# The last chunk's heads in other tiles, the rest behind the loop, paired convolution streams and another stage table, in a fused S4 convolution and multi-query attention kernel

## The chip, the cores and the metric

The kernel runs on one core of a Trainium2 chip. A core has a matmul engine (PE, with weight loads shown apart as PEld), a vector engine (DVE), an activation engine (ACT), a general engine (POOL) and a queue engine that mostly issues DMAs (SP). Each engine works through its own queue in program order; semaphores join them. Matmuls write to PSUM banks, everything else lies in SBUF or in DRAM. The metric is the device time of one execution in microseconds, the median of several runs.

## The reference

Two independent parts whose outputs are set side by side. Part A is a state-space (S4) convolution over 2048 positions and 576 channels; part B is attention with 32 heads of 18 columns that share one key and one value head.

```python
def _A_ref(u, A_re, A_im, B_re, B_im, C_re, C_im, log_dt, Dskip):
    ...
    P = jnp.exp(logdA[:, :, None] * l[None, None, :])
    K = jnp.einsum("dn,dnl,dn->dl", Cc, P, dB).real
    ...            # y: causal convolution of u with K, by FFT of length 2L
    return y + u * Dskip[None, None, :]

def _B_ref(x, wq, wk, wv, wo):
    ...            # q: 32 heads of 18; k, v: one head of 18
    scores = jnp.einsum("bhqd,bkd->bhqk", q, k) * (Dh ** -0.5)
    p = _softmax(scores, axis=-1)
    o = jnp.einsum("bhqk,bkd->bhqd", p, v)
    return o.transpose(0, 2, 1, 3).reshape(B, S, H * Dh) @ wo

return jnp.concatenate([a, b], axis=-1)
```

## The kernel before

**Attention** runs over 4 chunks (c) of 512 queries, in each over 8 groups (g) of 4 heads, in each over 16 key blocks (kb) of 128 keys: 512 steps. A step takes two pairs of heads: for each pair a score tile (`s`, two matmuls, L551) and one exponential on ACT (`P`, 128x1024, L562); then one *product* of four matmuls with the values (`ops`, L865), which also sums the softmax's denominators. Three score tiles (NS) and ten tiles of exponentials (NP) are in turn. After key block 15, `gather` copies the four heads to SBUF and stores them to `od` in DRAM (L571).

`normalize` turns a chunk's heads into normalised ones. For some of five column groups m (126 columns each, the last 72) it loads the denominators (`dn`, L584), takes reciprocals on DVE, stores them to `rden` (L588), loads the heads into tile `oT` (L591), loads the reciprocals broadcast over each head's 18 rows (`db`, L598) and multiplies (DVE). `outproj` then multiplies by `wo`: 8 sums (4 blocks of 128 queries by 2 column halves) over the five m. For the last chunk the projection is cut by m (`outproj_part`, after groups 1, 3, 5 and 6 by LATE): a sum over one m is taken in PSUM and collected by DVE in `part`. What is still in `self.rest` when the loop ends, and the last m by another route (`w4`, `b4`), is done by `finish`.

**The convolution** works through 12 blocks of 48 channels. `front(k)` builds tables of powers on DVE (`tab`) and from them the kernel on PE (`kg`, L1300), sent through DRAM (`kd`, `kt`). `back(k)` transforms input and kernel (`hu`, `lu`, `hk`, `lk`), multiplies on DVE (`acc`, `pt`), and transforms back (`iy`), after which block k is stored.

**What sets the order.** PE, ACT and DVE run in the order in which the program is written; DMAs on SP are placed by their dependences. `main` writes three scores, the exponentials, then products and *filler*: steps of four generators (`prep` for normalize, `tail`, `side` for query projections and outproj, and the convolution's streams). A clock inside the program (`K.t` for PE, `K.v` for DVE, `K.a` for ACT) estimates when each step could begin; `fill` takes those that fit before the next scores are due. The table `PLAN` gives the constants of this choice for each stage of 32 steps (RATE and PACE for the convolution's speed, TOTAL and LAST for how filler is spread over the steps, C1 to C12, and so on). A generator's `yield "v", t, ...` waits for that clock to reach t, `"p"` asks for PE, `"w"` waits for another generator. All filler sums go through one PSUM bank (`bank`), which DVE must empty before the next.

The places that the change touches: tile `oT` has one buffer, used by all chunks, so the last chunk waits in `prepare` until chunk 2's projection is done:

```python
            while ms[0] == 0 and (self.outs or c == NCH - 1 and self.due < 1 << 30):
                yield "w", 0.0, False
```

and the two convolution streams, `fronts` and `backs`, go on independently, where a stream that did vector work last goes first again:

```python
        for st in sorted(self.streams, key=lambda st: (not st.holds, st.kind == "v" and st is not self.on, st.work)):
```

Of the kernel before, what the change touches and what calls it, by code (L numbers as in the profile page):

```python
# [50 lines left out]
LAST = 405.243  # L51
# [3 lines left out]
    0: dict(RATE=1.916, PACE=1.819, AHEAD=0.674, TOTAL=358.207, GAP=0.333, DEFER=0.474, SLACK=3.538, HEAD=11.297, LEFT=1.367, C1=0.645, C2=0.912, C3=0.747, C4=1.053, C5=0.661, C6=1.093, C7=0.426, C8=0.221, C9=0.253, C10=0.689, C11=16.545, C12=15.321),  # L55
    1: dict(DEFER=0.444, SLACK=4.537, C10=0.575),
    2: dict(TOTAL=449.207, SLACK=4.082, HEAD=8.942),
    3: dict(RATE=1.877, TOTAL=358.207, SLACK=3.538, HEAD=11.297),
    5: dict(C11=19.186, C12=19.023),
    6: dict(RATE=1.952, C3=0.59, C4=1.266, C11=21.544),  # L60
    7: dict(RATE=1.916, C3=0.747, C4=1.053, C11=19.186),
    8: dict(LEFT=1.309, C5=0.644, C8=0.226, C9=0.311, C10=0.623),
    9: dict(RATE=1.906, DEFER=0.45, C3=0.831),
    10: dict(GAP=0.42, HEAD=12.368, C4=1.259, C8=0.182, C10=0.683),
    11: dict(RATE=1.916, GAP=0.291, DEFER=0.444, HEAD=13.273, C2=0.697, C3=0.747, C4=1.053, C8=0.208, C9=0.388, C10=0.557),
    12: dict(AHEAD=0.91, LEFT=1.367, C3=0.588, C5=0.661, C8=0.192, C9=0.316, C10=0.461),
    13: dict(AHEAD=0.701, GAP=0.333, C8=0.205, C9=0.332, C10=0.469),
    14: dict(PACE=1.844, AHEAD=0.86, C6=0.87),
    15: dict(RATE=1.869, PACE=1.922, AHEAD=0.657, GAP=0.384, DEFER=0.409, LEFT=1.696, C7=0.331, C8=0.169, C9=0.316, C10=0.408),
# [145 lines left out]
class Attention:  # L215
# [357 lines left out]
    def normalize(self, c, ms):  # L573
# [11 lines left out]
        yield "v", K.t + 8.0, False  # L585
# [3 lines left out]
        for m in ms:  # L589
            m0, mn = MT[m]  # L590
            nc.sync.dma_start(o[:mn, m, :], od[m0 // DH:(m0 + mn) // DH, 0:DH, :])  # L591
        yield "v", max(K.v, K.t) + 5.0, False
        tiles = {}

        def fetch(m):
            m0, mn = MT[m]
            tiles[m] = self.p1.tile([P, CT], F32, tag="db", name=f"db{c}_{m}", bufs=2)
            nc.sync.dma_start(tiles[m][:mn, :], rd[m0 // DH:(m0 + mn) // DH, :].unsqueeze(1).broadcast_to([mn // DH, DH, CT]))  # L598
        for m in ms[:2]:
            fetch(m)  # L600
        for m in ms:
            mn = MT[m][1]
            yield "v", K.t + 7.0, False
            V.tensor_tensor(o[:mn, m, :], o[:mn, m, :], tiles[m][:mn, :], op=ALU.mult)
# [4 lines left out]
    def outproj(self, c):  # L609
# [4 lines left out]
        for t in range(4):  # L614
# [17 lines left out]
            if t < 3:  # L632
                yield "p", K.fill, False

    def outproj_part(self, c, ms, part):

        nc, V, K = self.nc, self.V, self.k
        o = self.oT
        self.o_left += 8 * len(ms)
        for t in range(4):  # L640
            for n in range(2):
# [3 lines left out]
                for m in ms:  # L645
                    matmul4(nc, ps, o[:126, m, t * P:(t + 1) * P], self.wo[:126, m, cs], start=(m == ms[0]), stop=(m == ms[-1]))
# [13 lines left out]
    def finish(self, c, part, o_ps, w4, b4):  # L660


        nc, V, o = self.nc, self.nc.vector, self.oT
# [7 lines left out]
        def begin(t, nh, tile):  # L671

            ps[t, nh] = tile[:, :288]
            for m in range(4):
                if (t, nh, m) in self.rest:
                    matmul4(nc, ps[t, nh], o[:126, m, t * P:(t + 1) * P], self.wo[:126, m, cols[nh]], start=(m == min(x[2] for x in self.rest if x[:2] == (t, nh))), stop=False)
# [72 lines left out]
    def prepare(self):  # L749

        nc = self.nc
        while True:
# [5 lines left out]
            while ms[0] == 0 and (self.outs or c == NCH - 1 and self.due < 1 << 30):  # L758
# [3 lines left out]
            if c == NCH - 1 and ms[0] == 0:  # L762
                self.part = self.xp.tile([P, 4, D], F32, tag="x", name="part")
                self.rest = {(t, n, m) for t in range(4) for n in range(2) for m in range(4)}
            if ms[0] == 3:
                self.w4 = self.p1.tile([P, D], F32, tag="ob", name="w4")
# [857 lines left out]
```

## Time and profile before

| | |
|---|---|
| median of 3 runs | 1147.22 us (1146.74 to 1147.87) |
| the profiled execution, its own time | 1146.74 us |
| its span, first to last instruction | 1145.0 us |
| mean granted PE clock | 0.993 |
| first exponential begins / last ends | 25.9 us / 1109.0 us |
| exponentials | 1024, of 1036 ns (1121 ns for the first 32) |

The page has the busy share of each engine, the span in 40 slices, the chain of work that ended last, and the costliest groups of instructions; the trace behind it answers for any stretch. In a group's row stand line, engine, operation, `out<-in` by the program's names, count, then busy time and mean length of one, then the engine's idle time before it and what ended that. In a row of stretches stand the busy times of PE, PEld, DVE, ACT and POOL with their counts of instructions, the granted PE clock, the DMA share and GB/s. A matmul in 32-bit floats stands twice in the records. Idle time of an engine costs only where another waits for it.

```profile
PE   6989999999999999899999999999999999999986
DVE  3878998899999998999899999996998999994823
ACT  3889988988898999999899989999899999999970
```

### The profile page before, as it was taken

What the parts mean: (1) busy time and instruction counts of PE and PEld (TensorE: products, weight loads), DVE (VectorE), ACT (ScalarE), POOL (GpSimd) and SP (SyncE); (2) the same over time, 40 slices, a digit from 0 to 9 for tenths busy, and PEclk for the clock granted to TensorE, in tenths of its full rate; (3) what the DMA queues carried; (4) which work ended last, traced back from release to release, by engine and by line L of the source; (5) the groups of instructions that cost most, each with busy time, mean ns of one, the idle gap of its engine ahead of it and who ended that gap; (6) DMA issues with size and microseconds to landing.
All of it is one profiled execution on the core that took longest, in us unless ns stands there. A gap on an engine that the chain in (4) does not pass through costs nothing.

```text
span 1145.0 us, 33016 instructions
## 1 busy us (share of the span) xinstructions
PE 1082.4 (95%) x13886; PEld 395.8 (35%) x13886; DVE 991.3 (87%) x1676; ACT 997.1 (87%) x1052; POOL 139.5 (12%) x257
## 2 busy tenths in 40 slices
PE   6989999999999999899999999999999999999986
PEld 2333333334334333333333233333333233333323
DVE  3878998899999998999899999996998999994823
ACT  3889988988898999999899989999899999999970
POOL 5333212412122100000102010000020000000000
PEclk9999999999999999999999999999999999999997
DMA  7424142312214103031303112012132102011201
GB/s 225 142 58 125 40 146 62 113 42 82 62 58 158 43 22 103 20 111 37 108 29 124 46 34 87 29 38 71 40 128 72 59 23 95 29 43 43 79 34 53
DMA packets 59279, 83.37 MB, mean 73 GB/s; under 512 B 14867, under 2 KB 35335, under 8 KB 58613
## 3 DMA queue, kind: packets, MB, share of 16 engines
q1 hardware_dynamic: 47557, 73.24, 19.6%
q0 software_dynamic: 10848, 7.37, 2.6%
q8 instruction: 111, 1.82, 0.7%
q10 hardware_dynamic: 720, 0.58, 0.2%
q14 instruction: 43, 0.35, 0.1%
HBM read 46.59 MB, written 33.85 MB: 70 GB/s over the span
## 4 chain that ended last, share of the span: by engine, by line
PE 64%; ACT 14%; DVE 13%; issue 5%; DMA 2%; POOL 0%; SPq 0%; DVEq 0%; ACTq 0%
PE ops L865 26%; PE s L551 18%; ACT P L562 13%; PE op L212 5%; PE iy L212 3%; PE q L428 3%; PE kg L1300 2%; DVE tab L138 2%; DVE acc L138 1%; PE hk L212 1%; PE lu L212 1%; DVE ks L138 1%; PE fin L212 1%; PE hu L212 1%; DVE t L138 1%
## 5 line engine op out<-in xcount | busy, mean ns | idle before, releaser
L562 ACT ACTIVATE P<-s 128x1024 f32<-128x1024 f32 x992 | 933.1, 1036 | 88.1 <-PE s L551 86.0
L865 PE MATMUL ops<-P,v_sb 128*32 128x512 f32 x4096 | 504.1, 595 | 4.4 <-DVE o L142 4.0
L551 PE MATMUL s<-aug,kaug 55*128 55x512 f16 x2048 | 309.9, 380 | 25.6 <-ACT P L562 19.0
L551 PEld LDWEIGHTS <-kaug 55*128 55x128 f16 x2048 | 93.2, 94 | 352.8 <-issue 304.6
L865 PEld LDWEIGHTS ops<-P,v_sb 128*32 128x32 f32 x4096 | 117.0, 110 | 165.6 <-issue 136.4
L479 POOL DMA_DIRECT2D qd<-qh x116 | 66.1, 576 | 321.6 <-DVE qh L146 319.0
L428 PE MATMUL q<-x,wq_sb 128*32 128x256 f32 x1360 | 83.7, 383 | 1.2 <-issue 1.2
L212 PE MATMUL op<-wo_sb,oT 126*32 126x288 f32 (+1 forms) x1024 | 74.7, 418 | 2.8 <-DVE ob L142 1.6
L1211 POOL MEMSET fr<- 128x192 f32 x24 | 9.9, 494 | 442.5 <-DVE stage L138 237.8
L138 DVE TENSOR_TENSOR tab<-tab,tt 128x576 f32<-128x576 f32 (+1 forms) x72 | 59.2, 822 | 2.0
L138 DVE TENSOR_TENSOR tab<-fr,dif 128x576 f32<-128x576 f32 (+1 forms) x72 | 58.8, 817 | 0.0
L138 DVE TENSOR_TENSOR tab<-sum,fr 128x576 f32<-128x576 f32 (+1 forms) x72 | 58.7, 816 | 0.0
L138 DVE TENSOR_TENSOR tt<-fr,sum 128x576 f32<-128x576 f32 (+1 forms) x72 | 58.7, 816 | 0.0
L138 DVE TENSOR_TENSOR tab<-tab 128x576 f32<-128x576 f32 (+1 forms) x72 | 58.7, 815 | 0.0
L428 PEld LDWEIGHTS q<-x,wq_sb 128*32 128x32 f32 x1360 | 39.7, 109 | 37.2 <-issue 15.5
L138 DVE TENSOR_TENSOR acc<-acc,pt 128x1728 f32<-128x1728 f32 (+2 forms) x36 | 48.6, 1350 | 0.6
L138 DVE TENSOR_TENSOR pt<-us,ks 128x1728 f32<-128x1728 f32 (+2 forms) x36 | 47.8, 1350 | 0.2
L560 ACT ACTIVATE P<-s,bias 128x1024 f32<-128x1024 f32 x32 | 32.9, 1121 | 13.4 <-PE s L551 13.4
L1300 PEld LDWEIGHTS kg<-tab 128*32 128x32 f32 x2304 | 36.1, 110 | 21.1 <-issue 9.8
L1300 PE MATMUL kg<-tab 128*32 128x64 f32 x2304 | 41.8, 220 | 0.2
L138 DVE TENSOR_TENSOR ks<-ks 128x576 f32<-128x576 f32 (+1 forms) x48 | 41.0, 855 | 1.0
L212 PEld LDWEIGHTS op<-wo_sb,oT 126*32 126x32 f32 (+1 forms) x1024 | 29.1, 111 | 36.2 <-issue 13.4
(159 smaller groups left out, 995.0 us busy)
## 6 DMA issues: line engine op xcount, KB each, us to landing
od<-o SPq DMA_DIRECT2D x31, 256.0 KB
aug<-qd SPq DMA_DIRECT2D x124, 55.0 KB
u<-u SPq DMA_DIRECT2D x12, 384.0 KB
kd<-ksb SPq DMA_DIRECT2D x12, 384.0 KB
kt<-kd SPq DMA_DIRECT2D x48, 96.0 KB
outa<-u SPq DMA_DIRECT2D x12, 384.0 KB
pw<-pw SPq DMA_DIRECT2D x8, 528.0 KB
oT<-od SPq DMA_DIRECT2D x16, 252.0 KB
```

The source lines that it names most:

```text
L138: return self.v.tensor_tensor(out, *a, **k)
L212: nc.tensor.matmul(ps[j:e], w[:, j:e], x, start=start, stop=stop, tile_position=(0, j))
L428: nc.tensor.matmul(ps[o, 256 * f:256 * f + 256], w[:, k, i], xt[:, k, x], start=(k == 0), stop=(k == 4), tile_position=(0, 32 * j))
L479: q.dma_start(qd[h:h + n, row + d:row + d + nd, cs], src[i1:i1 + n * nd, :cs.stop - cs.start])
L551: nc.tensor.matmul(ps[:, j, :], self.kaug[r, kb * P:(kb + 1) * P], t[r, :], start=True, stop=True)
L560: nc.scalar.activation(pt, ps, AF.Exp, bias=self.bias, scale=SCALE / QQ)
L562: nc.scalar.activation(pt, ps, AF.Exp, scale=SCALE / QQ)
L865: nc.tensor.matmul(o_ps[32 * j:32 * j + 32, :], self.v[:, kb, :], pts[2 * n + j // 2][:, j % 2, :], start=(kb == 0), stop=(kb == 15), tile ...
L1211: nc.gpsimd.memset(t[:, :, 0:NF:8], one)
L1300: nc.tensor.matmul(ps[32 * g:32 * g + 32, d, :], t[:, :32], t[:, 32:], start=(j == 0), stop=(j == 1), tile_position=(0, 32 * g))
```

## The change

Four edits.

1. **Heads.** The last chunk's heads are no longer kept in `oT` but in the first four tiles of the query weights (`self.heads`, 512 columns of `wq[0]` to `wq[3]`), which are free once the last query projection is done. So the last chunk's normalisation waits for the queries alone, not for chunk 2's projection. `w4` is loaded when chunk 2's projection has been written. The waits in `normalize` are other ones: they reckon from the gather and from the time of the fetch.
2. **Behind the loop.** What is left after the last product is written in the order in which its inputs come by the program's clock.
3. **Streams in pairs.** Back of block k and front of block k + 1 make a pair of streams; the next pair begins when both are done. No stream keeps its turn.
4. **Stage table.** PLAN and LAST have other numbers.

```diff
-LAST = 405.243
+LAST = 576.841
...
-    0: dict(RATE=1.916, PACE=1.819, AHEAD=0.674, TOTAL=358.207, GAP=0.333, DEFER=0.474, SLACK=3.538, HEAD=11.297, ...
+    0: dict(RATE=1.86, PACE=1.856, AHEAD=0.729, TOTAL=340.0, GAP=0.359, DEFER=0.395, SLACK=3.285, HEAD=17.08, ...
...
-LAG = (0, -1)
...
@@ normalize
-        if ms[0] == 0:
-            self.oT = self.cp.tile([P, 5, CT], F32, tag="oT", name=f"oT{c}")
-        o = self.oT
+        if c < NCH - 1:
+            oT = self.oT = self.cp.tile([P, 5, CT], F32, tag="oT", name=f"oT{c}")
+            o = [oT[:, m, :] for m in range(5)]
+        else:
+            o = self.heads
...
-        yield "v", K.t + 8.0, False
+        yield "v", max(K.t + 1.0, self.o_free + 4.5) + 4.0, False
...
-        yield "v", max(K.v, K.t) + 5.0, False
-        tiles = {}
+        yield "v", max(K.v, K.t) + 1.6, False
+        tiles, fetched = {}, {}
...
-            yield "v", K.t + 7.0, False
+            yield "v", max(K.t, fetched[m] + 4.6), False
...
@@ outproj, at its end
+        if c == NCH - 2:
+            self.w4 = self.p1.tile([P, D], F32, tag="ob", name="w4")
+            nc.sync.dma_start(self.w4, self.a["wo4"])
...
@@ prepare
-            while ms[0] == 0 and (self.outs or c == NCH - 1 and self.due < 1 << 30):
+            while ms[0] == 0 and (self.outs if c < NCH - 1 else self.due < 1 << 30):
...
+                self.heads = [w.rearrange("p k n -> p (k n)")[:, :CT] for w in self.wq[:4]]
...
@@ main, behind the last product
-        while self.todo or self.busy or holder() or any(m == 0 for _, _, m in self.rest):
+        while True:
+            conv.turn()
+            h, live = holder(), [st for st in conv.streams if st.live]
             if self.todo or self.busy:
-                prep.advance()
-            elif holder() or self.outs:
-                (holder() or side).advance()
-        conv.drain()
+                live.append(prep)
+            if side.holds or self.outs and any(m == 0 for _, _, m in self.rest):
+                live.append(side)
+            if not live:
+                break
+            able = [st for st in live if st.kind == "v" or st.kind == "p" and h in (None, st)]
+            for st in [min(able, key=lambda st: st.event())] if able else live:
+                if st.live:
+                    K.t = max(K.t, st.event())
+                    st.advance()
...
@@ Conv
+    def turn(self):
+
+        if self.n < NCK and not any(st.live for st in self.streams):
+            self.n += 1
+            k = self.n
+            self.streams = [Stream(self.back(k, self.kt), self.k)] if k < NCK else []
+            if k + 1 < NCK:
+                self.streams.append(Stream(self.front(k + 1), self.k))
...
-        for st in sorted(self.streams, key=lambda st: (not st.holds, st.kind == "v" and st is not self.on, st.work)):
+        for st in sorted(self.streams, key=lambda st: (not st.holds, st.work)):
```

How the order of instructions moves, at three places.

On PE, from the last two products to the sums behind them. `fin` are the sums of `finish`, `bc` the broadcast of the last group's reciprocals; x24 are the 24 matmuls of six sums. Before:

```order
L865 MATMUL ops3_7_13947<-P3_14_15_14199,v_sb_115 32x512 x2
L865 MATMUL ops3_7_13947<-P3_15_15_14220,v_sb_115 32x512 x2
L212 MATMUL fin0_14263<-wo_sb_107,oT3_13810 32x288 x24
L704 MATMUL bc_14262<-rc_last_14261,b4_14246 128x256
L212 MATMUL fin1_14264<-wo_sb_107,oT3_13810 32x288 x24
L212 MATMUL fin2_14265<-wo_sb_107,oT3_13810 32x288 x24
L212 MATMUL fin0_14263<-w4_14245,o_last_14260 32x288 x8
L212 MATMUL fin3_0_14353<-wo_sb_107,oT3_13810 32x288 x12
```

Of the change:

```order
L869 MATMUL ops3_7_14039<-P3_14_15_14306,v_sb_115 32x512 x2
L869 MATMUL ops3_7_14039<-P3_15_15_14334,v_sb_115 32x512 x2
L211 MATMUL fin0_14358<-wo_sb_107,wq3_sb_105 32x288 x8
L211 MATMUL fin1_14359<-wo_sb_107,wq3_sb_105 32x288 x8
L211 MATMUL fin2_14360<-wo_sb_107,wq3_sb_105 32x288 x4
L709 MATMUL bc_14357<-rc_last_14356,b4_14032 128x256
L211 MATMUL fin2_14360<-wo_sb_107,wq3_sb_105 32x288 x4
L211 MATMUL fin0_14358<-w4_13157,o_last_14355 32x288 x8
L211 MATMUL fin3_0_14400<-wo_sb_107,wq3_sb_105 32x288 x4
```

Sums over m = 1 and m = 2 (16 of them) are gone from here; they stand as `op3_..._1` and `op3_..._2` in the last 23 groups of three scores.

On DVE, the last rows before the last group's reciprocal (`rc_last`). Before, with `db3_1` to `db3_3` the broadcast reciprocals of m = 1 to 3:

```order
L138 TENSOR_TENSOR oT3_13810<-oT3_13810,db3_1_14201 126x512
L146 TENSOR_SCALAR dn3_14_14235<-dn3_14_14235 28x128
L158 RECIPROCAL dn3_14_14235<-dn3_14_14235 28x128
L138 TENSOR_TENSOR oT3_13810<-oT3_13810,db3_2_14242 126x512
L146 TENSOR_SCALAR dn3_21_14249<-dn3_21_14249 28x128
L158 RECIPROCAL dn3_21_14249<-dn3_21_14249 28x128
L138 TENSOR_TENSOR oT3_13810<-oT3_13810,db3_3_14256 126x512
L938 TENSOR_SCALAR flag_58<-u2_3_4_11177 1x1
L693 TENSOR_SCALAR rc_last_14261<-ops3_7_13947 128x256
```

Of the change:

```order
L137 TENSOR_TENSOR wq3_sb_105<-wq3_sb_105,db3_3_14150 126x512
L137 TENSOR_TENSOR part_11912<-part_11912,op3_2_1_2_14216 128x288
L137 TENSOR_TENSOR w11_14185<-sv11_14184 128x2x192 x4
L137 TENSOR_TENSOR part_11912<-part_11912,op3_3_0_2_14245 128x288
L137 TENSOR_TENSOR u11_12556<-u11_12556,dsk11_12557 128x768
L137 TENSOR_TENSOR u11_12556<-u11_12556,iy110_14271 128x384
L137 TENSOR_TENSOR u11_12556<-u11_12556,iy111_14308 128x384
L137 TENSOR_TENSOR part_11912<-part_11912,op3_3_1_2_14340 128x288
L952 TENSOR_SCALAR flag_58<-u2_3_4_8890 1x1
L698 TENSOR_SCALAR rc_last_14356<-ops3_7_14039 128x256
```

The last head multiply moves ahead of the end of convolution block 11, and block 11's inverse transform (`iy11`), which stood ahead of the last fifteen products, now ends ahead of the last four.

On DVE, where block 10's products and block 11's tables meet. Before:

```order
L138 TENSOR_TENSOR pt10_2_13070<-us10_12300,ks10_12550 128x576
L138 TENSOR_TENSOR acc10_13004<-acc10_13004,pt10_2_13070 128x96x12
L138 TENSOR_TENSOR acc10_13004<-acc10_13004,pt10_2_13070 128x96x6
L138 TENSOR_TENSOR acc10_13004<-acc10_13004 128x768 x2
L138 TENSOR_TENSOR sv10_13128<-acc10_13004 128x384
L138 TENSOR_TENSOR sv10_13128<-acc10_13004 128x2x192
```

Of the change:

```order
L137 TENSOR_TENSOR acc10_13126<-acc10_13126,pt10_2_13305 128x96x6
L137 TENSOR_TENSOR tab11_1_13340<-sum11_12848,fr11_12677 128x24x24
L137 TENSOR_TENSOR acc10_13126<-acc10_13126 128x768
L141 COPY part_11912<-op3_2_0_0_13392 128x288
L137 TENSOR_TENSOR tt11_1_0_0_13343<-fr11_12677,sum11_12848 128x576
L137 TENSOR_TENSOR acc10_13126<-acc10_13126 128x768
L137 TENSOR_TENSOR tab11_1_13340<-tab11_1_13340 128x24x24
```

Rows of block 10 (`acc10`) and block 11 (`tab11`, `tt11`) now alternate, and a sum of the last chunk's projection (`part`) already stands among them.

More of the change, by code (lines that the diff above doesn't have):

```diff
@@ L1470, in early @@
         self.load(0)
[L1471 to L1482 removed]
+        self.n, self.burst = -1, False
+        self.streams = [Stream(self.front(0), self.k)]
     def begin(self, n):
@@ L1520, in drain @@
     def drain(self):
-        while any(st.live for st in self.streams):
-            for st in sorted(self.streams, key=lambda st: (not st.holds, st.kind == "w", st.work)):
+        while self.streams:
+            for st in sorted(self.streams, key=lambda st: (not st.holds, st.work)):
                 if st.live:
@@ L1525, in drain @@
                     break
+            self.turn()
 def build(tc, **aps):
```

72 lines of the change are left out of this document (29 added, 43 removed).

## The prediction

> **What bounds the kernel now.** First the page's head and its busy shares.
>
> ```profile
> span 1145.0 us, 33016 instructions
> PE 1082.4 (95%) x13886; PEld 395.8 (35%) x13886; DVE 991.3 (87%) x1676; ACT 997.1 (87%) x1052; POOL 139.5 (12%) x257
> ```
>
> No engine is the bound alone, and PE's 95% is not 5% of slack, because matmul ends are modelled. An average over the span hides where each is short, so I went to stretches: I cut the span at the first exponential of each 32 steps (64 exponentials a stage) and asked for each engine's busy time. Columns are start and end, length, then PE, PEld, DVE, ACT and POOL busy with their counts, granted clock, DMA share, GB/s. Four of the sixteen stages, and the sum of all:
>
> ```profile
> 242.40:314.20 71.80, 68.76 (x986) 27.02 (x987) 67.76 (x121) 60.46 (x66) 16.12 (x29) 1.00 0.24 69
> 381.80:445.20 63.40, 61.22 (x763) 21.21 (x752) 59.97 (x91) 59.98 (x66) 2.26 (x4) 1.00 0.15 45
> 853.60:914.30 60.70, 56.19 (x678) 18.08 (x678) 55.35 (x97) 59.55 (x65) 7.01 (x13) 1.00 0.21 67
> 1044.90:1109.00 64.10, 61.62 (x634) 19.89 (x635) 36.72 (x55) 60.16 (x64) 0.00 (x0) 1.00 0.15 50
> sum 1083.00, PE 1043.41 PEld 381.20 DVE 971.69 ACT 989.65 POOL 127.22; mean PE 65.21 PEld 23.83 DVE 60.73 ACT 61.85 POOL 7.95
> ```
>
> ACT needs about 60 us for any stage, and the lightest stage (853.6) takes hardly more. What a stage takes beyond that is ACT waiting for scores, because PE was busy with, or held up in, the other matmuls ("filler"). Over the loop this is 1083.0 - 989.65 = **93 us**. DVE is short in the early stages (67.76 of 71.80) and idles 27 us in the last (36.72 of 64.10).
>
> The loop's last exponential ends at 1109.0; the other 36 us lie behind it. Pieces of the chain in order of time (start, us, what) from there:
>
> ```profile
> 1108.08 1.35 DMA rden<-dn
> 1109.45 4.10 DMA db<-rden
> ...
> 1116.73 4.05 DMA db<-rden
> ...
> 1121.62 3.49 PE fin L212 x32
> 1125.12 0.63 PE bc L704 x2
> 1125.74 8.39 PE fin L212 x136
> ```
>
> The last chunk's heads of column groups m = 2 and m = 3 are normalised one after the other, each by a reciprocal, a store to DRAM and a broadcast load, while PE has nothing: `fin` cannot begin in earnest before 1121.62. Then 32 partial sums of the output projection, 24 of them over m = 1 to 3, run in the open.
>
> **The change part by part.** Times are against the profiled execution: span 1145.0, and 1.7 us around it (its own time is 1146.74; the median of the three runs, 1147.22, is 0.5 above). The rows of the end, from the timeline (start, us, engine, line):
>
> ```profile
> 1107.80 2.78 PE L865 MATMUL ops<-P,v_sb 128*32 128x512 f32 x24
> 1121.54 0.40 DVE L693 TENSOR_SCALAR rc_last<-ops 128x256 f32<-128x256 f32 x1
> 1121.98 1.75 DVE L696 RECIPROCAL rc_last<-rc_last 128x256 f32<-128x256 f32 x1
> 1125.78 0.42 DVE L690 TENSOR_TENSOR o_last<-o_last,bc 128x256 f32<-128x256 f32 x1 [1.77 <-PE bc L704]
> 1134.69 1.18 PE L212 MATMUL fin<-w,o_last 128*32 128x288 f32 x16
> 1138.49 1.55 DVE L682 TENSOR_TENSOR part<-part,fin 128x288 f32<-128x288 f32 x4 [1.74 <-PE fin L212]
> ```
>
> *1. Heads in their own tiles.* The last product ends at 1107.80 + 2.78 = 1110.6, so the tail is 1145.0 - 1110.6 = 34.4 us. In the change each m of the last chunk is normalised when its columns' groups are gathered, since it no longer waits for chunk 2's projection to leave oT; the multiply for m = 3 stands on DVE ahead of conv block 11's last transform, and `fin` holds 8 sums instead of 24. So the two round trips leave the tail, and 16 sums move into the loop. The new tail, from the end of the last product: DVE clamp 0.40 and reciprocal 1.75 (2.2; PE runs 5 sums of 0.49 beside it, 8.39 us for 136 records being 17 sums), bc 0.63, scale 0.42, the second reciprocal 1.75, bc 0.63, with some 0.4 of hand-over: 6.0. From there the rows of before run 1134.69 to 1140.04 = 5.35 with three sums in `begin(3,1)` where one is left (less 1.1): 10.25. From the last addition to the span's end before: 1145.0 - 1140.04 = 4.96. New tail **15.2, saved 19.2**. What is late next is DVE's pair of reciprocals, not PE.
>
> The saving includes a slow stretch of PE. By stretches:
>
> ```profile
> 1114.20:1124.40 10.20, 3.97 (x32) 1.39 (x36) 4.23 (x8) 0.74 (x2) 0.00 (x0) 0.50 0.08 27
> ```
>
> The granted clock was 0.50 there, behind the idle of 1111 to 1114, and 4 sums took 3.49 where four at 0.49 take 2.0. Without the idle I expect none of it.
>
> *2. The 16 sums in the loop.* Prices by the groups of the trace (busy over count, doubled, because a matmul stands twice in the records):
>
> ```profile
> L428 PE MATMUL q<-x,wq_sb 128*32 128x256 f32 x1360 | 83.7, 383 | 1.2 <-issue 1.2
> L212 PE MATMUL op<-wo_sb,oT 126*32 126x288 f32 (+1 forms) x1024 | 74.7, 418 | 2.8 <-DVE ob L142 1.6 <-DVE sck L138 1.2
> L1300 PE MATMUL kg<-tab 128*32 128x64 f32 x2304 | 41.8, 220 | 0.2
> L212 PE MATMUL iy<-w,dft_sb 128*32 128x192 f32 x768 | 37.3, 329 | 0.6 <-DVE ql L150 0.6
> L212 PE MATMUL hk<-kt,dft_sb 128*32 128x192 f32 x384 | 21.1, 331 | 1.6 <-DVE ql L150 0.8 <-DVE sck L138 0.5 <-PE s L551 0.3
> ```
>
> A sum of four is 8 records of op: 74.7 / 1024 x 8 = 0.58, so 16 are 9.3 us more filler in the loop. Bounds: nothing, if they fall where ACT is not kept waiting, and 9.3. The stages give the slope. Counted in the order and priced so, the filler of stage 242.4 was 25.4 us and ACT idled 71.80 - 60.46 = 11.3; stage 853.6 had 9.3 and idled 60.70 - 59.55 = 1.2; stage 381.8 had 14.8 and idled 3.4. From the first to the second that is 0.63 per us, thus +5.9; bent at the third it is 0.40 below 14.8 us and 0.75 above. **3. The stage table** shifts filler along that bend: by the same count stage 242.4 falls from 25.4 to 18.5 and stage 776.8 from 26.9 to 17.7, while stage 853.6 rises from 9.3 to 14.8 and the last from 14.8 to 23.2. Of the 9.3 us more, then, 5.5 lie below the bend (x 0.40) and 3.8 above it (x 0.75), together **+5**, which I take; 0 to 9.3 are the bounds.
>
> *4. Streams in pairs.* Back of block k runs beside front of k + 1 and neither keeps its turn, so DVE alternates between the two. From the DVE timeline:
>
> ```profile
> 1022.07 0.95 DVE L138 TENSOR_TENSOR tab<-fr,dif 128x768 f32<-128x768 f32 x1
> 1022.93 0.95 DVE L138 TENSOR_TENSOR tab<-sum,fr 128x768 f32<-128x768 f32 x1
> ...
> 1025.14 0.95 DVE L138 TENSOR_TENSOR tab<-tab 128x768 f32<-128x768 f32 x1
> 1026.12 0.96 DVE L138 TENSOR_TENSOR tab<-tab,tt 128x768 f32<-128x768 f32 x1
> ```
>
> Start to start is 0.86 where the next reads another tile and 0.98 where it reads the tile just written: 0.12 for the dependence. The order has 494 such neighbours before and 448 now: 46 x 0.12 = 5.5 us off DVE. Against it stand 16 additions into `part` at 1.55 / 4 = 0.39: 6.2. DVE's sum stays (+0.7); I count 0, bounds -2 to +3. [...]
>
> *5. Block 11 at the end.* Its transform back (iy11) now ends four products before the end instead of fifteen. Its chain before, from the DVE timeline:
>
> ```profile
> 1049.16 0.56 DVE L142 COPY sck<-hk 128x384 f32<-128x384 f32 x1 [2.80 <-PE hk L212]
> ...
> 1053.44 0.56 DVE L142 COPY sck<-hk 128x384 f32<-128x384 f32 x1 [1.72 <-PE hk L212]
> 1056.70 1.02 DVE L138 TENSOR_TENSOR sck<-lk,sck 128x384 f32<-128x384 f32 x2 [2.70 <-PE lk L212]
> ...
> 1080.51 1.00 DVE L138 TENSOR_TENSOR w<-sv 128x384 f32<-128x384 f32 x2
> ...
> 1113.57 0.69 DVE L138 TENSOR_TENSOR oT<-oT,db 126x512 f32<-126x512 f32 x1 [5.51 <-DMA db<-rden]
> ```
>
> From 1049.16 (its first kernel transform's copy) to 1081.5 (its last w) took 32.3 us with 4.4 us of waiting in it; that leaves 28 of work, to which the change adds ten additions (1.55 / 4 each: 3.9) and two head multiplies (0.69 each): 33.2. Between the same two places the new order has 36 exponentials, at 60.16 / 64 = 0.94 each 33.8 us. It fits with nothing to spare; PE waits in order at iy11. I add **+1**, bounds 0 to 8.
>
> *6. At no cost.* The dn, rden and db transfers of m = 0 to 2 lie under the loop; the new waits of the planner (8.5 us from gather to dn, 6.2 from reciprocal to multiply) cover the 5.45 us of the chain's first round (1.35 + 4.10). Without cover DVE waits for them, rival D. The new loop behind the last product finds no matmul left to place. w4 goes out earlier on SP. Sum: 1145.0 - 19.2 + 5 + 0 + 1 = 1131.8 span, **1133.5** with the 1.7.
>
> **The rivals.** *A, the forecast:* 1133.5, 1127 to 1141 by the bounds of parts 2 and 4. *B, DVE is relieved early:* block 11 ends 11 of 512 products later, so 2% of the 971.69 us of DVE work, some 20 us, leaves the first fourteen stages. If ACT's idle there falls by 0.4 of it, the loop is 8 us shorter: 1125.5. For it speaks that stages with DVE near its length idle most; against it that filler alone explains those stages. *C, DVE late at the end:* each addition frees the one filler bank, and the conv's long multiplies stand in front of some. If part 5 takes its 8 instead of 1: 1140.5. [...] *D, slower:* DVE, in order, stands at head multiplies whose broadcast has not landed, as it did 5.51 us ahead of the one at 1113.57. The place is the 19 multiplies in four chunks, where x of chunk 3 or block 11's kd and kt go out on SP ahead of a broadcast. The gain of 13.7 us on the median is gone when each waits 13.7 / (19 x 0.63) = 1.1 us; at 1.5 it is 1133.5 + 18 = 1151.5. The margins above speak against it. *E, the change doesn't do it:* m = 2 and m = 3 are normalised behind the loop all the same. Then the 11 us from 1110.6 to 1121.62 stay, and 8 sums more in the loop give about what they save behind it: 1147. The order speaks against it.
>
> **How the numbers follow.** A 0.58, B 0.15, C 0.17, D 0.05, E 0.05. Predicted is A's 1133.5. The range, 1121 to 1143, takes in A's bounds, most of B and C's worst; about 0.2 are outside. A measurement tells 0.2% (2.3 us) here: faster, below 1144.9, is A, B and nearly all of C: 0.89; same E: 0.05; slower D and a rest of C: 0.06.
>
> **What would show it.** Right: no DVE or PE wait for db behind the last product, a tail of 15 to 16 us, no stretch of granted clock 0.50 at the end, ACT idle of 93 to 103 us between first and last exponential. Wrong: DVE idle "<-DMA db" inside the loop (D); PE idle at iy ahead of the last products (C); ACT idle well under 93 (B).

## The result and the profile after

| | before | changed |
|---|---|---|
| median | 1147.22 us (1146.16 to 1150.87, 5 runs) | 1139.79 us (1136.86 to 1140.67, 5 runs) |
| ratio | | 0.9931, 95% interval 0.9914 to 0.9949 |
| the profiled execution, and its span | 1146.74, 1145.0 us | 1140.67, 1138.9 us |
| first exponential begins | 25.9 us | 26.8 us |
| loop, first to last exponential | 1083.1 us | 1094.2 us |
| behind the last exponential | 36.0 us | 17.9 us |

The change makes the kernel 0.7% faster, where 1.2% was forecast (1133.5 us). The profiled execution is the slowest of the five. Behind the last exponential 18.1 us are gone; reckoned from the last product, as the forecast reckons, it is 18.6 of the 19.2 forecast. The loop is longer by 11.1 us instead of 6, and that is where the rest of the gain went.

The page's head:

```profile
span 1138.9 us, 33011 instructions
PE 1080.4 (95%) x13886; PEld 395.6 (35%) x13886; DVE 992.7 (87%) x1692; ACT 998.9 (88%) x1052; POOL 140.0 (12%) x257
```

The work is the same (16 more DVE instructions, the additions). The stretches of 64 exponentials that answer to those shown of before, the last two stages, and the sum:

```profile
246.90:314.90 68.00, 63.87 (x882) 23.35 (x882) 61.08 (x114) 59.94 (x64) 12.21 (x22) 1.00 0.23 67
385.80:452.80 67.00, 64.82 (x816) 23.21 (x812) 63.86 (x97) 60.27 (x65) 0.00 (x0) 1.00 0.12 37
858.10:921.10 63.00, 59.52 (x764) 21.20 (x767) 53.68 (x97) 59.97 (x66) 0.81 (x2) 1.00 0.23 75
986.50:1054.70 68.20, 66.88 (x808) 23.41 (x804) 66.14 (x113) 60.77 (x66) 0.00 (x0) 1.00 0.15 48
1054.70:1121.00 66.30, 65.62 (x846) 24.45 (x847) 50.37 (x82) 60.69 (x64) 0.00 (x0) 1.00 0.15 49
sum 1094.20, PE 1050.76 PEld 385.14 DVE 975.26 ACT 991.55 POOL 128.25; mean PE 65.67 PEld 24.07 DVE 60.95 ACT 61.97 POOL 8.02
```

The stage that lost filler is shorter (71.80 to 68.00), those that got it are longer (63.40 to 67.00, 60.70 to 63.00, 64.10 to 66.30), in the direction that the forecast gives. The size fits for one of them (60.70 to 63.00, where 5.5 us more filler at 0.40 make 2.2) and not for the last: there 8.4 us more at 0.75 would make 6.3, and it took 2.2. ACT stands 1094.20 - 991.55 = 102.65 us in the loop, 93 before. By stages, 6.7 of the 11.1 us lie in the first fourteen, which hold no sum of the last chunk, and 2.2 in each of the last two.

The end, from the timeline (start, us, engine, line):

```profile
1121.20 1.90 PE L869 MATMUL ops<-P,v_sb 128*32 128x512 f32 x16
...
1122.91 2.61 PE L211 MATMUL fin<-wo_sb,wq_sb 126*32 126x288 f32 x40
...
1123.62 1.75 DVE L701 RECIPROCAL rc_last<-rc_last 128x256 f32<-128x256 f32 x1
...
1126.57 1.75 DVE L714 RECIPROCAL rc_last<-rc_last 128x256 f32<-128x256 f32 x1
...
1131.83 1.55 DVE L687 TENSOR_TENSOR part<-part,fin 128x288 f32<-128x288 f32 x4 [0.77 <-PE fin L211]
```

and the last pieces of its chain (start, us, what):

```profile
1123.10 2.43 PE fin L211 x40
1125.52 0.67 PE bc L709 x2
1126.19 2.18 PE fin L211 x32
1128.37 0.70 PE bc L715 x2
1129.07 2.74 PE fin L211 x40
```

No `rden` and no `db` is left behind the last product, which ends at 1121.20 + 1.90 = 1123.1. The tail is 1138.9 - 1123.1 = 15.8 us; before it was 34.4. The granted clock (third figure from the end) stays at 1.00 there:

```profile
1121.00:1133.00 12.00, 11.74 (x156) 5.06 (x148) 8.13 (x16) 0.79 (x3) 0.00 (x0) 1.00 0.17 59
```

### The profile page after: what moved, and what is told of

Read it like the earlier page. It is cut to its first block, busy times and chain, and to the rows that moved or that the text cites. A ratio compares the mean times of both kernels' runs of the same rounds, so it can differ in the third digit from the quotient of the medians.

```text
span 1138.9 us, 33011 instructions
## 1 busy us (share of the span) xinstructions
PE 1080.4 (95%) x13886; PEld 395.6 (35%) x13886; DVE 992.7 (87%) x1692; ACT 998.9 (88%) x1052; POOL 140.0 (12%) x257
## 3 DMA queue, kind: packets, MB, share of 16 engines
q8 instruction: 111, 1.82, 0.7%
## 4 chain that ended last, share of the span: by engine, by line
PE 59%; DVE 21%; ACT 10%; issue 6%; DMA 3%; POOL 1%; DVEq 0%; SPq 0%; ACTq 0%
PE ops L869 24%; PE s L550 15%; ACT P L561 9%; PE op L211 5%; DVE tab L137 5%; PE kg L1314 3%; DVE ks L137 3%; PE iy L211 3%; PE q L427 2%; DVE acc L137 2%; DVE tt L137 1%; PE hu L211 1%; PE hk L211 1%; DVE pt L137 1%; DMA db<-rden 1%
## 5 line engine op out<-in xcount | busy, mean ns | idle before, releaser
L869 PE MATMUL ops<-P,v_sb 128*32 128x512 f32 x4096 | 509.5, 599 | 3.0 <-DVE o L141 2.8
L211 PE MATMUL op<-wo_sb,oT 126*32 126x288 f32 (+1 forms) x960 | 67.5, 410 | 2.5 <-DVE ob L141 2.5
L141 DVE COPY ksb<-kg 128x192 f32<-128x192 f32 x48 | 17.3, 360 | 41.5 <-PE kg L1314 41.5
```

Source lines behind the costliest of these rows:

```text
L141: return self.v.tensor_copy(out, *a, **k)
L211: nc.tensor.matmul(ps[j:e], w[:, j:e], x, start=start, stop=stop, tile_position=(0, j))
L869: nc.tensor.matmul(o_ps[32 * j:32 * j + 32, :], self.v[:, kb, :], pts[2 * n + j // 2][:, j % 2, :], start=(kb == 0), stop=(kb == 15), tile ...
```

## The experiments

Each is run beside the kernel before on the same chip; the ratio is to that kernel. First a table of all, then each with its edit.

| kernel | median us | ratio, 95% interval |
|---|---|---|
| the change | 1139.79 | 0.9931 (0.9914 to 0.9949) |
| the change with old waits | 1161.10 | 1.0123 (1.0102 to 1.0145) |
| the change, 16 sums behind the loop | 1147.14 | 0.9988 (0.9966 to 1.0011) |
| the change with the old table | 1160.65 | 1.0112 (1.0087 to 1.0137) |
| the change with the old streams | 1165.02 | 1.0156 (1.0139 to 1.0173) |
| the change without the 16 sums | 1136.96 | 0.9911 (0.9894 to 0.9928) |
| the change without waits for db | 1139.01 | 0.9931 (0.9916 to 0.9947) |
| the change with useless matmuls in two gaps | 1142.36 | 0.9956 (0.9939 to 0.9973) |
| before with edit 1 (heads) alone | 1138.80 | 0.9917 (0.9901 to 0.9934) |
| before with edit 4 (table) alone | 1159.74 | 1.0089 (1.0060 to 1.0118) |
| before with edit 3 (pairs) alone | 1182.64 | 1.0302 (1.0275 to 1.0329) |
| heads alone, more filler at the end, A | 1137.41 | 0.9897 (0.9878 to 0.9916) |
| heads alone, more filler at the end, B | 1135.55 | 0.9897 (0.9871 to 0.9922) |

### One part of the change undone

**Old waits.**

```diff
-        yield "v", max(K.t + 1.0, self.o_free + 4.5) + 4.0, False
+        yield "v", K.t + 8.0, False
...
-        yield "v", max(K.v, K.t) + 1.6, False
+        yield "v", max(K.v, K.t) + 5.0, False
...
-            yield "v", max(K.t, fetched[m] + 4.6), False
+            yield "v", K.t + 7.0, False
```

> The change with the old waits of the planner in normalize (8 us, 5 us and 7 us by its clock instead of the shorter ones). The order still has 8 sums of m = 0, 1 and 2 each in the loop, so the tail stays 15.8 us. Theory (short waits cost the loop): in the profile of the change DVE stands 1.42 and 1.16 us for db at 339 to 343 us, PE then stands 2.59 us for a table and runs 3.4 us at a granted clock of 0.50. With the old waits DVE never waits for db inside the loop and these 4 to 6 us go: 1134 to 1136 us. Rival (the short waits are hidden or needed): the planner only reshuffles, 1139 to 1141 us, with as many stretches of clock 0.50 in the loop (three).

Measured: 1161.1 us, 21 over the change; both theories missed it. DVE no longer waits for `db` in the loop, but only the first four stages are as in the change, and everything behind has another order. The loop is 21 us longer. The wait of PE that grew most (us in total, times, longest), in the change and then in this kernel:

```profile
PE ops L869 <- DVE o L141: 2.8, 5, 1.3
```

```profile
PE ops L869 <- DVE o L141: 17.1, 11, 5.2
```

The product of a new group waits until DVE has copied the heads of the last one out of PSUM. The longest of these waits is here, in this kernel's timeline:

```profile
861.19 3.66 DVE L137 TENSOR_TENSOR stage<-stage,m 128x792 f32<-128x792 f32 x4 [6.48 <-ACT stage L1182]
...
876.81 0.68 DVE L141 COPY o<-ops 128x512 f32<-128x512 f32 x1
```

DVE came to `stage` before ACT's sines, stood 6.48 us in order, and the heads' copy, 15 us of DVE work further on, came late. So this run does not price the waits: it measures another order, under a table that came with a different one.

**The 16 sums behind the loop.**

```diff
-            elif ms[0] < 3:
+            elif ms[0] < 1:
                 self.begin_output(self.outproj_part(c, ms, self.part))
```

> The change, but the 16 sums over m = 1 and m = 2 stay behind the loop. The tail grows by 16 x 0.49 = 7.8 us, to 23 to 24 us. Theory (a sum in the loop costs half its 0.58 us, +5 in all): the loop shortens by 4 to 6 us, time 1141 to 1144 us. Rival 1 (the sums cost all of their 9.3 us, which explains the loop's +11): the loop shortens by 9 us or more, time 1137.5 to 1139 us. Rival 2 (the sums in the loop cost nothing, its +11 is stalls and clock): loop as in the change within 2 us, time 1146 to 1148 us.

Measured: 1147.1 us. The loop took 1095.4 us against the change's 1094.2, the stretch behind it 24.3 against 17.9. Taking the sums out did not shorten the loop, as rival 2 had it. But it is not the price of the sums: in the last stage a head multiply of DVE now came ahead of its broadcast, and PE then waited for DVE:

```profile
1079.38 0.69 DVE L137 TENSOR_TENSOR wq_sb<-wq_sb,db 126x512 f32<-126x512 f32 x1 [3.02 <-DMA db<-rden]
```

```profile
1081.46 0.86 PE L211 MATMUL lk<-kt,dft_sb 128*32 128x192 f32 x16 [2.70 <-DVE sck L141]
```

This is the forecast's rival D, in the open: the last stage took 67.2 us here, and 64.2 in a kernel (below) that has the 16 sums left out and hardly another difference in its order. The price of the sums is read from that one.

**Old table, and old streams**, in two kernels: PLAN and LAST as before, and the class Conv as before.

```diff
-LAST = 576.841
+LAST = 405.243
...
```

> The change with the stage table of the kernel before. By its order 13 of the 16 sums go back behind the loop (21 partial sums of m = 1 to 3 there instead of 8), so the tail grows by 13 x 0.49 = 6.4 us to about 22 us. Theory (the table's worth is that it lets the sums into the loop, and little else): the loop shortens by 13/16 of 5 us, time 1141 to 1144 us. Rival (the table by itself evens out the filler and is the larger part of the gain): loop no shorter than that of the change, time 1146 to 1149 us.

```diff
+    def fronts(self):
+        for k in range(NCK):
+            yield from self.front(k)
...
     def turn(self):
-
-        if self.n < NCK and not any(st.live for st in self.streams):
...
+        pass
...
```

> The change with the two independent convolution streams of the kernel before (a stream keeps its turn). Neighbours on DVE that read the tile just written rise from 448 to 492, 44 x 0.12 = 5.3 us more DVE work. Theory (forecast's part 4: hidden, since DVE is short nowhere for long): within 3 us of the change, 1137 to 1143 us, DVE's sum up by 5 us. Rival 1 (DVE work counts at 0.6): 1143 us and more. Rival 2 (pairs hurt, since both streams then wait for PE: DVE waits 41.5 us for kg in the change, 18.5 before): 1133 to 1137 us.

Measured: 1160.7 and 1165.0 us, 21 and 25 over the change, beyond every theory on record but the second's open "1143 and more". Loops of 1109.1 and 1111.1 us. PE's wait for the heads' copy is 6.1 and 10.1 us where the change has 2.8. Three edits of different kinds, each with its own meaning, and each time 21 to 25 us: what they have in common is that the order changes in the first third of the loop and the table came with another order. That the table is the cause is argued from this, not shown: no table was made anew for any of them.

### The change in its own order

In the next three nothing that the planner counts is changed, so that the rows of all engines stay where they were but for the edit (and a few rows that changed places). The first leaves the 16 sums out, so that part of the output is missing; the second scales the heads of chunks 0 to 2 by other numbers than their reciprocals.

**Without the 16 sums.**

```diff
-                ps = self.bank(288, f"op{c}_{t}_{n}_{ms[0]}")
+                if ms[0] == 0:
+                    ps = self.bank(288, f"op{c}_{t}_{n}_{ms[0]}")
+                else:
+                    K.pe(0.0, K.fill)
                 for m in ms:
-                    matmul4(nc, ps, o[m][:126, t * P:(t + 1) * P], self.wo[:126, m, cs], start=(m == ms[0]), stop=(m == ms[-1]))
+                    if m == 0:
+                        matmul4(nc, ps, o[m][:126, t * P:(t + 1) * P], self.wo[:126, m, cs], start=(m == ms[0]), stop=(m == ms[-1]))
...
-                    V.tensor_tensor(part[:, t, cs], part[:, t, cs], ps, op=ALU.add)
+                    K.dve(part[:, t, cs], 1.04e-3, part[:, t, cs])
```

> The change in its own order, but the 16 sums over m = 1 and m = 2 of the last chunk are left out (their 64 matmuls and 16 additions; nothing is put in their place, the part of the output that they make is missing). It gives their price in the loop with every other row where it was. Theory after the run with the sums behind the loop (they fill holes that block 11's chain on DVE leaves anyway): loop shorter by 0 to 2 us, time 1138 to 1140 us. Rival 1 (the forecast's price): shorter by 5, time 1135 us. Rival 2 (full price): shorter by 9.3, time 1130.5 us.

Measured: 1136.96 us, 0.9911 against 0.9931: 2.3 us by the ratios, 2.8 by the medians, with intervals that overlap. The last two stages of this kernel, at full clock as in the change, show it better:

```profile
982.90:1050.90 68.00, 65.96 (x790) 22.93 (x787) 65.94 (x113) 60.68 (x66) 0.00 (x0) 1.00 0.15 49
1050.90:1115.10 64.20, 60.72 (x736) 21.54 (x739) 45.41 (x68) 60.26 (x65) 0.00 (x0) 1.00 0.15 51
```

68.20 + 66.30 became 68.00 + 64.20: **the sums cost 2.3 us, 0.14 each**, a quarter of their 9.3 us on PE; a little over the theory (0 to 2) and half of the forecast's 5. PE's time falls by 5.8 us in these two stages, the stages by 2.3; the rest was time in which PE would have stood. Behind the loop the same 16 make 16 x 0.49 = 7.8 by PE's rows; in the run with them there, the tail from the last product was 22.8 us, 7.0 over the change's.

**Without the waits for db.**

```diff
+            by = tiles[m][:mn, :] if c == NCH - 1 else self.wo[:mn, m, :CT]
-            V.tensor_tensor(o[m][:mn, :], o[m][:mn, :], tiles[m][:mn, :], op=ALU.mult)
+            V.tensor_tensor(o[m][:mn, :], o[m][:mn, :], by, op=ALU.mult)
```

> The change in its own order, but the head multiplies of chunks 0 to 2 read the output weights, long loaded, instead of the broadcast reciprocals, so DVE cannot wait for those (15 of 19 multiplies; output differs). Theory (rival D of the forecast is there once, at 340 us): DVE's waits of 3.1 us, PE's gap of 2.59 us at 343 us and mostly the clock of 0.50 behind it go, time 1135 to 1138 us. Rival (hidden): 1139 to 1140.5 us.

The place in the change, from its timeline:

```profile
340.84 0.69 DVE L137 TENSOR_TENSOR oT<-oT,db 126x512 f32<-126x512 f32 x1 [1.42 <-DMA db<-rden]
342.69 0.69 DVE L137 TENSOR_TENSOR oT<-oT,db 126x512 f32<-126x512 f32 x1 [1.16 <-DMA db<-rden]
...
345.64 0.88 PE L1314 MATMUL kg<-tab 128*32 128x64 f32 x48 [2.59 <-DVE tab L137]
```

and in this kernel:

```profile
350.07 0.28 DVE L145 TENSOR_SCALAR sh<-u 8x256 f16<-8x256 f32 x1 [4.96 <-DMA qd<-sh]
...
352.60 1.93 PE L427 MATMUL q<-x,wq_sb 128*32 128x256 f32 x16 [3.62 <-DVE ksb L141]
```

Measured: 1139.0 us, ratio 0.9931 as the change's. The waits went, and DVE stood 4.96 us at its next instruction that waits for a transfer (`sh`, for `qd`), where in the change it stood 0.54. The rival was right: the wait for `db` was hidden in front of this one. DVE's waits for `db` and `qd` are 3.1 + 4.7 = 7.8 us in all in the change and 8.7 here, for `qd` alone. PE has a gap of 3.62 us behind it.

**Useless matmuls in two of PE's gaps.** Of the change's three stretches of granted clock 0.50, two begin 1.3 and 1.9 us behind a gap of PE (2.19 and 2.59 us; the stretches begin at 135.91 and 347.54). Does the stretch go when the gap is filled, and does the time fall? That both would was the author's guess.

```diff
...
+        for _ in range({"up1_0": 9, "kg3_0_0": 11}.get(name, 0)):
+            self.nc.tensor.matmul(ps, self.kaug[0:55, 0:P], self.kaug[0:55, 0:CT], start=True, stop=True)
```

> The change in its own order, with 9 useless matmuls of 512 columns (0.2 us each) put into PE's gap of 2.19 us at 132.5 us and 11 into that of 2.59 us at 343.1 us, into the bank that the next sum overwrites. [...]

The two places in its timeline:

```profile
134.63 2.85 PE L243 MATMUL up<-kaug 55*128 55x512 f16 x9 [2.10 <-DVE ql L149]
...
346.73 2.54 PE L243 MATMUL kg<-kaug 55*128 55x512 f16 x11
```

Measured: 1142.4 us, 2.6 over the change by the medians, though the intervals of the ratios overlap a little. At the first place the gap stayed (2.10 us): the useless matmuls need nothing but the filler bank, so that is what PE waits for there, until DVE has read it (`ql`); they came behind the gap, in front of the scores, and took 2.85 us for nine, with 1.92 for the eight of `ops` behind them, where at the second place eleven took 2.54 and eight of `ops` 1.06 (stage 75.2 to 78.8 us). At the second the gap went, and the rows behind it are as long as at a clock of 1.00 (48 of `kg` 0.88 us, six of the scores 0.82), but the stage took 70.8 us, in the change 70.9. Here the stretch cost nothing that shows. So the first gap was not filled, and filling the second brought no gain: the guess is not borne out.

### One part alone on the kernel before

**Heads alone** (the diff's edit 1 without the waits).

```diff
+            o = self.heads
...
-            while ms[0] == 0 and (self.outs or c == NCH - 1 and self.due < 1 << 30):
+            while ms[0] == 0 and (self.outs if c < NCH - 1 else self.due < 1 << 30):
```

> The kernel before with edit 1 alone (the last chunk's heads in the query weights' tiles, w4 loaded after chunk 2's projection; old waits, old streams, old table). By its order 23 partial sums stay behind the loop instead of 24, and no head multiply stands behind the last product but the last. Theory 1 (the round trips leave the tail whatever the table): tail 22 to 24 us instead of 34.4, loop within 3 us of before, time 1134 to 1138 us. Theory 2 (a table fits one order only; any edit without a new table costs 13 to 20 us in the loop, as in three runs above): tail the same 22 to 24 us, loop longer by 13 to 20 us, time 1150 to 1157 us.

Measured: 1138.8 us, ratio 0.9917 beside the change's 0.9931: **edit 1 alone is worth as much as all four.** At the same mean granted clock of 0.994 it took 1138.7 and 1138.9 us, the change 1140.5 and 1140.7; that is a hint that the rest of the change costs something, from two runs each. Its first and last stage, and its end:

```profile
26.20:106.60 80.40, 75.12 (x970) 29.19 (x970) 65.03 (x133) 64.85 (x67) 24.84 (x45) 0.92 0.31 92
...
1051.80:1114.50 62.70, 59.46 (x678) 20.12 (x678) 38.95 (x62) 59.87 (x64) 0.00 (x0) 1.00 0.15 47
```

```profile
1113.79 2.76 PE L869 MATMUL ops<-P,v_sb 128*32 128x512 f32 x24
1116.37 2.61 PE L212 MATMUL fin<-wo_sb,wq_sb 126*32 126x288 f32 x40
...
1119.58 6.03 PE L212 MATMUL fin<-wo_sb,wq_sb 126*32 126x288 f32 x96
```

The tail is 1138.9 - 1116.55 = 22.4 us instead of 34.4, with 23 sums in it and no round trip. The loop took 1088.3 us, 5.2 over before, of which 4.4 are the first stage, where this execution ran at a clock of 0.92 (of the four runs it is the slowest, 1140.70). Stages 2 to 12 are as before within 0.1 us; the order there is untouched. Theory 1 held in the tail; the time lies 0.8 us over its range, and the loop of this execution 2.2 us, less than the 4.4 of its first stage at a clock of 0.92.

**Table alone, pairs alone:** PLAN and LAST of the change, and the class Conv of the change.

```diff
-LAST = 405.243
+LAST = 576.841
...
```

> The kernel before with edit 4 alone (the new PLAN and LAST). By its order PE's rows change from the 140th on, 16 partial sums instead of 24 stay behind the loop. Theory (a table fits the order that it was fitted for): loop longer by 10 to 25 us, time 1153 to 1168 us. Rival (the table evens out filler for any order, forecast's part 3): 1143 to 1148 us.

```diff
+    def turn(self):
...
```

> The kernel before with edit 3 alone (streams in pairs, old table). PE's rows change from the 748th on; dependent neighbours on DVE fall from 494 to 472, 22 x 0.12 = 2.6 us. Theory (any early change of the order under a table made for another costs 13 to 20 us): 1155 to 1168 us. Rival 1 (forecast's part 4, nothing either way): 1144 to 1149 us. Rival 2 (pairs save as they spare DVE 2.6 us): 1143 to 1146 us.

Measured: 1159.7 and 1182.6 us. Their loops take 1106.5 and 1103.0 us, 23 and 20 more than before. The table's time is within its theory; the pairs' is 15 us over theirs, because there the end grew too: 50.0 us lie behind the last exponential, which ends at 1129.24. Of the chain from 1116 on:

```profile
1116.16 4.21 DMA db<-rden
1123.57 3.66 DMA db<-rden
1130.47 3.98 DMA db<-rden
1137.63 4.15 DMA db<-rden
```

Chunk 2's projection came later (its last results leave at 1102.5, before at 1066.3), so tile oT was free later, and four round trips lie in the chain, two of them begun ahead of the last exponential, where before has two. DVE's waits for `db` are 21.7 us instead of 11.0: the same cost that edit 1 takes away, doubled. No run tests edit 2, the order behind the loop, by itself.

### Edit 1 and more filler at the end

Edit 1 alone leaves 23 sums behind the loop at 0.49 us. Two kernels, A and B, put 11 of them into the last stages and change nothing earlier. Of B:

```diff
-    14: dict(PACE=1.844, AHEAD=0.86, C6=0.87),
+    14: dict(PACE=1.844, AHEAD=0.86, C6=0.87, RATE=1.95, C3=1.0, C4=1.5),
...
-                urgent = self.due < self.step + 8
+                urgent = self.due < self.step + 8 or self.step >= 480 and self.outs and len(self.rest) > 16
```

> The kernel before with edit 1 alone, and in the last two stages of its table more filler (RATE 2.0, C3 1.2, C4 2.0) and, from step 488, sums of the last chunk's projection ahead of the convolution until 12 are left. By its order 12 partial sums of m = 1 to 3 stay behind the loop where edit 1 alone leaves 23, and block 11's transform back ends ahead of the last five products. Theory (a sum costs 0.49 us behind the loop and 2.3 / 16 = 0.15 us in the loop, where PE stands anyway): 11 x 0.34 = 4 us under edit 1 alone, 1134 to 1136 us. Rival (block 11 and the sums crowd DVE and the one filler bank in the last stage): loop longer by 4 us or more, 1138 to 1142 us.

> The same with a milder table (RATE 1.95, C3 1.0, C4 1.5) and the sums first from step 480 until 16 are left: 12 partial sums behind the loop too, the sums earlier, block 11's transform back later (ahead of the last two products). Theory: 1134 to 1136 us. Rival (a late block 11 holds up PE at its transforms): 1138 us and more.

Measured: 1137.4 and **1135.55 us, both 0.9897**. B's interval, 0.9871 to 0.9922, meets the change's (0.9914 to 0.9949) at its edge. Its last two stages and the sum:

```profile
978.00:1046.30 68.30, 66.81 (x900) 24.16 (x892) 64.08 (x98) 60.32 (x65) 0.00 (x0) 1.00 0.11 38
1046.30:1113.30 67.00, 64.50 (x686) 21.36 (x686) 39.33 (x63) 60.05 (x64) 0.00 (x0) 1.00 0.14 46
sum 1087.00, PE 1047.37 PEld 382.14 DVE 977.89 ACT 989.47 POOL 127.89; mean PE 65.46 PEld 23.88 DVE 61.12 ACT 61.84 POOL 7.99
```

Behind the last exponential B takes 20.4 us, 4.0 less than edit 1 alone; the last stage gives back 67.00 - 62.70 = 4.3 in these two executions. A is the cleaner comparison, since its profiled execution has its stretches of half clock at the same places as that of edit 1 alone (from 30.1, 71.1 and 808.3 us); the spans are 1139.2 and 1138.9 us. Its last two stages:

```profile
983.80:1052.20 68.40, 66.84 (x900) 24.29 (x891) 63.95 (x98) 60.37 (x65) 0.00 (x0) 1.00 0.11 38
1052.20:1120.70 68.50, 65.75 (x714) 21.92 (x715) 39.51 (x65) 60.26 (x65) 0.00 (x0) 1.00 0.15 51
```

Edit 1 alone took 68.00 and 62.70 there. So A pays 6.2 us in the loop for 5.9 saved behind it, as the rival had it, though its median lies under the rival's range. Neither kernel bears out the price of 0.15 us for a sum in the loop: it holds for the 16 sums in the change's order and not for these 11, which came with a later block 11. B's median, 3.2 us under that of edit 1 alone (2.3 by the ratios), goes with its clock: its two runs at 0.993 and 0.995 took 1140.0 and 1140.4 us, edit 1 alone at 0.994 took 1138.7 and 1138.9. A gain is not shown.

## Why the forecast was right in direction, and off in size

Forecast and measurement differ by 7.1 us of span (1131.8 and 1138.9): 0.9 before the first exponential, 5.1 in the loop (11.1 for 6) and 1.1 behind it.

*Part 1, the heads: right.* Tail 15.2 forecast, 15.8 measured; no stretch of 0.50 ahead of the last sums (granted clock 1.00 from 1121 to 1133 us). What is late next was to be DVE's reciprocals; the chain shows PE's `fin` and `bc`, which fill 1123 to 1132. It is a near tie: the two reciprocals end at 1125.37 and 1128.32, and the broadcasts that need them begin on PE at 1125.52 and 1128.37. Edit 1 alone confirms the step: the tail falls by 12.0 us by it, and the time by as much as with the whole change.

*Part 2, the 16 sums: mechanism right, mis-sized.* +5 was taken, the run without them gives 2.3. The slope was taken over all stages, but the sums stand in the last, where DVE idled 27 us of 64 and PE stood too. This error ran against the next one: with 2.3 in place of 5 the loop would have been forecast 3.3 us longer, not 6, against 11.1. That the time came out as near as it did is in part luck.

*Part 3, the table, and part 4, the pairs: the term that failed.* They were put at an even trade and at 0 (bounds -2 to +3). The run without the 16 sums has the change's order in the first fourteen stages and not one stretch of clock 0.50. Those stages before, with one stretch, and in that run:

```profile
25.90:978.90 953.00, 916.56 (x11948) 337.07 (x11951) 879.01 (x1498) 869.03 (x915) 127.32 (x232) 1.00 0.23 73
26.80:982.90 956.10, 914.04 (x11939) 336.87 (x11938) 858.61 (x1462) 869.97 (x914) 127.59 (x232) 1.00 0.23 72
```

So this order is 3 us or a little more longer than the old one, not equal; the profiled execution of the change, with three stretches, took 959.7. The forecast read filler per stage, which does explain which stages grew and which shrank, but not their sum. What it left out is PE standing for DVE: in these stages PE's waits for DVE are 11.7 us before and 17.9 in that run. Most of the rise is at `up` and `kg` (7.7 us for 0.9); the wait for the heads' copy, which the runs with another order show, is no part of it (3.0 for 4.0). How much of this reaches ACT is not shown. Whether pairs by themselves gain or lose is open: both ways of testing them ran under a table that came with another order.

*Part 5, block 11: about right.* The last two stages are 4.4 us longer; 2.3 are the sums; some 2 remain for the late block and whatever else the table moved there, where +1 was taken (0 to 8). No run separates these.

*Part 6, the waits: right in cost, not in cover.* The waits did not cover every round trip: DVE waits three times for `db` in the loop, 3.1 us. Without them the time is the same, because the next wait takes it back, which the forecast did not reckon with. In the run with the sums behind the loop one such wait was not hidden.

*The rivals.* B fell, though its premise came true: DVE's work in the first fourteen stages fell by 20.3 us (879.01 to 858.75 in the change), and the stages grew all the same. C fell: PE is busy 65.62 of 66.30 us in the last stage and stands 0.0 us at `iy`. D happened in the change, at 340 us above all, and was hidden by the next wait. E fell by the profile of the end.

*Not in the sum: the clock.* The forecast counted one stretch of half clock, at the end. The profiled execution of the change has three in the loop, before had one. The three stages that hold them took 75.50, 75.20 and 70.90 us, and 74.50, 75.00 and 69.60 in the run without the sums, which has none: 2.5 us together.

## What to carry to other kernels

Where a table of constants belongs to one order, test an edit by one that leaves the order as long as possible, or without touching what the planner counts: five edits that changed it in the first third all cost 12 to 35 us, whatever they meant. That a table made anew would win this back was not tried. Take the serial round trips out of the end first; here that alone was the gain (a ratio of 0.9917, with everything else 0.9931). And look at the next instruction that waits for a transfer before you count a wait that is removed: here 3.1 us of DVE's waits for `db` went, and DVE stood 4.96 us at the next one, where it had stood 0.54. Look also where the wait stands: one of 3.0 us for the same kind of broadcast, in the last stage, held up PE by 2.7.

## What the runs showed of the hardware

In the traces the places where the granted clock falls to 0.50 lie on a grid of 3.413 us. Windows of the change (columns as above; the clock is the third from the end):

```profile
26.69:30.10 3.41, 2.23 (x15) 0.87 (x14) 2.83 (x17) 3.31 (x4) 3.41 (x8) 1.00 0.24 56
30.10:33.51 3.41, 3.41 (x16) 0.58 (x14) 0.98 (x6) 3.41 (x4) 3.41 (x8) 0.50 0.40 83
132.50:135.91 3.41, 1.26 (x18) 0.36 (x20) 3.38 (x6) 3.40 (x4) 1.84 (x4) 1.00 0.02 5
135.91:139.32 3.41, 3.41 (x18) 0.84 (x18) 3.34 (x8) 3.05 (x4) 3.41 (x7) 0.50 0.33 84
344.13:347.54 3.41, 1.63 (x54) 0.96 (x54) 3.38 (x6) 1.03 (x2) 1.83 (x4) 1.00 0.51 167
347.54:350.95 3.41, 3.07 (x40) 0.92 (x40) 2.84 (x9) 2.26 (x3) 1.07 (x2) 0.50 0.30 86
88.12:91.53 3.41, 1.82 (x76) 1.22 (x80) 2.31 (x6) 2.11 (x4) 3.19 (x6) 1.00 0.60 145
```

The stretches of 0.50 begin at 30.10, 135.91 and 347.54 and last 3.41 us. The first and the last lie 317.44 us apart, 93 x 3.4133; the distances from each to the next are 31.00 and 62.00 times that. Each follows a window in which PE was busy 1.26 to 2.23 of 3.41 us. So PE stood 1.2 to 2.2 us in the window ahead of each. The busy share alone doesn't settle when a stretch comes: the window at 88.12, busy 1.82, had none behind it, and the one at 26.69, busy 2.23, had. What brings a stretch on is therefore open.

In each of the eleven executions where two or more beginnings were measured, of this kernel and the others, these lie at the same place modulo 3.4133 us, to 0.02 us; from one execution to the next that place lies anywhere from 0.5 to 2.8 us. Each kernel has only one trace, so that the grid's place also differs between runs of one kernel, and with it the count of stretches, is inferred; the mean granted clock of such runs does differ, and their times go with it. In the five runs of the change the granted clock was 0.997, 0.996, 0.995, 0.994 and 0.994 with 1136.86, 1138.66, 1139.79, 1140.45 and 1140.67 us; in ten runs of the kernel with the sums behind the loop the four at 0.989 to 0.992 took 1149.3 to 1151.3 us, the four at 0.996 1142.1 to 1144.4. A single profile of such a kernel can lie 4 us off its best run (1140.67 and 1136.86 here). That the clock is the cause is not shown; in the run with the useless matmuls a stretch less made no difference to its stage.
